# Last Fourier stage in column tiles, spectral products taken from PSUM, one-bank tiles and merged score units, in a kernel that mixes segmented attention with a Fourier filter

## Chip, cores, metric

One core of a Trainium2 chip. The time is the device time of one execution in microseconds (us), lower is better. Engines: PE is TensorE (matmuls), PEld its weight loads, DVE is VectorE, ACT is ScalarE, POOL is GpSimd, SP issues the DMAs. "Granted clock" is the TensorE clock that the throttle let through, as a share of full speed. The state of a run is fast or slow (over 1.5% above the fastest run of the same kernel).

## The reference, cut to what matters

```python
def reference(A_x, A_wq, A_wk, A_wv, A_wo, A_beta, B_x, B_w_r, B_w_i, gate_w):
    # x: (1, 2048, 640) bf16; 32 heads of 20; 4 segments of 512 tokens
    g = sigmoid((x * gate_w).sum(-1, keepdims=True))
    a = _A_ref(x, ...)   # per segment: causal softmax attention inside the segment, mixed with
                         # phi(q) @ M / (phi(q) @ z), where M, z sum phi(k)^T v and phi(k) of the
                         # segments before; phi(t) = t + 1 if t > 0 else exp(t); then @ wo
    b = _B_ref(x, w_r, w_i)  # irfft2(rfft2(x) * (w_r + i w_i)), cast to bf16
    return g * a + (1 - g) * b
```

Two independent computations share the core. Attention has 4 segments x 8 groups of four heads: scores, `exp`, a causal mask, times v. The Fourier part is a chain of matmul stages (called F1, D, T, the product with W, Tb, Db, Fb in the code). The two meet only in the last line.

## The kernel before

The kernel records all its operations, each with a priority in planned microseconds. A list scheduler then plays an execution with estimated costs and fixes the order of each engine's queue and which PSUM bank each tile takes. So a constant in `texp` or `F_START` is not a delay on the chip: it decides what stands in front of what in each in-order queue. PSUM has two pools: banks 0 to 3 are one score tile ("qk"), banks 4 to 7 are for everything else.

```python
    TSTART, TEND = 14.0, 232.0          # planned times of the first and last score unit
    F_START, F_END = 18.0, 160.0        # planned times of the Fourier part
    def texp(self, s, g, u=0):
        return self.TSTART + ((s * 8 + g) * 3 + u) / 96.0 * (self.TEND - self.TSTART)
# ... one group of four heads: three score units, each through the one four-bank tile
            for u, js in enumerate(((0,), (1, 3), (2,))):     # widths 512, 512, 256 per head
                bank = Bank(4, "qk")
                # ... 4 or 8 qk matmuls (row tiles), then
                self.one("act", lambda e: e.activation(ex..., self.ps(bank, 0, [512, 4], [1, width]), ACT.Exp, scale=SC), ...)
                for j in js:
                    self.one("pool", lambda e: e.affine_select(...), 512, ...)      # causal mask
# ... phi: exp on ACT; min(.,1) and max(.,0) and the add on POOL or DVE, whichever the scheduler finds free
            self.Sc.op({"pool": (fmax,) + ts, "dve": (fmax,) + tsd}, ...)
            self.Sc.op({"pool": (fmin,) + ts, "dve": (fmin,) + tsd}, ...)
            self.Sc.op({"pool": (fadd, ...), "dve": (fadd, ...)}, ...)
# ... Fourier part, group g of 16: T in PSUM -> copy to SBUF (Xt) -> products with W on DVE or POOL
                self.Sc.op(self.copy_alts(Xt.ap(ri * 322, [1, KD]), self.ps(bank, 0, [1, KD]), KD), ..., name="ev_T")
            for r in range(2):
                fn = lambda e: e.tensor_tensor(Pt.ap(r * 644, [322, 2], [1, KD]), Xt.ap(0, [322, 2], [1, KD]),
                                               Wt.ap(r * 322, [0, 2], [1, KD]), ALU.mult)        # 642 wide
                self.Sc.op({"dve": (fn, ...), "pool": (fn, ...)}, ..., name="W_mul")
# ... last stage, token residue n2 of 16: full 128-column matmuls give tokens n2, n2+16, n2+32, ...
                for typ in range(2):
                    return (self.ps(bank, 0, [1, 320]), fc.ap(384 if hf and typ else 256, [1, P]),
                            Gt.ap(typ * 322 + 320 * hf, [1 - 2 * hf, 320]), typ == 0, typ == 1, {})
            self.dma(yd[n2::16], ys, ..., name="st_y")           # y to DRAM, strided by 16 tokens
# ... out tile T_ of 128 consecutive tokens
        self.dma(yl, yd[T_ * 128 : ...], [all 16 yd], ..., name="ld_y")    # y back, in token order
        self.one("pool", lambda e: e.tensor_scalar(yl, yl, (1 - g) column, None, ALU.mult), D, ..., name="y_scale")
        # ... 2 x 5 output-projection matmuls, then on DVE: out = psum * g + yl; store
```

(Argument lists, priorities and dependencies are left out where `...` stands.)

The softmax here doesn't subtract the row's maximum and nothing guards it: scores larger than these inputs give would overflow.

Of the kernel before, what the change touches and what calls it, by code (L numbers as in the profile page):

```python
# [10 lines left out]
ALU = mybir.AluOpType  # L11
# [39 lines left out]
class Sched:  # L51
# [9 lines left out]
    def op(self, alts, r=(), w=(), prio=0.0, nbytes=0, name="", tr=False):  # L61
# [14 lines left out]
        for b in r2:  # L76
            dep(b.w)
        for b in w2:
            bb = b
            if isinstance(b, Bank):  # L80
                o.banks.append(b)
                b.ops.append(o)
                bb = b.buf
            dep(bb.w)
            for q in bb.r:
                dep(q)
# [398 lines left out]
class Kern:  # L485
# [56 lines left out]
    def one(self, eng, fn, n, r, w, prio, per=None, fix=None, name=""):  # L542
        fix0, per0 = {"act": (100, 0.833), "dve": (75, 1.04), "pool": (130, 0.86)}[eng]
        per = per0 if per is None else per
        fix = fix0 if fix is None else fix
        return self.Sc.op({eng: (fn, fix + per * n, 90.0)}, r=r, w=w, prio=prio, name=name)

    def dma(self, dst, src, nbytes, r, w, prio, tr=False, name=""):
        def f(e):
            d_, s_ = dst(), src()  # L550
            if tr:
                return e.dma_start_transpose(d_, s_)
            with self.nc.allow_non_contiguous_dma(reason="small strided loads"):
                return e.dma_start(d_, s_)
        return self.Sc.op({"sp": (f, 450.0, 0.0)}, r=r, w=w, prio=prio, nbytes=nbytes, name=name, tr=tr)


    TSTART = 14.0
    TEND = 232.0
    F_START = 18.0  # L560
    F_END = 160.0

    def texp(self, s, g, u=0):
        return self.TSTART + ((s * 8 + g) * 3 + u) / 96.0 * (self.TEND - self.TSTART)

# [13 lines left out]
    def alloc(self):  # L579
# [6 lines left out]
        self.yd = nc.dram_tensor("y_scr", (S, D), BF)  # L586
# [4 lines left out]
        self.Ac = T("Ac", [P, 5 * 2048])  # L591
# [6 lines left out]
        self.Xt = [T(f"Xt{i}", [P, 2 * 322]) for i in range(2)]  # L598
        self.Pt = [T(f"Pt{i}", [P, 4 * 322]) for i in range(1)]
# [3 lines left out]
        late = [self.Ac.off]  # L603

        def TL(name, shape):
# [3 lines left out]
            assert late[0] <= self.fcat.off  # L609
            return t  # L610
        self.Gt = [TL(f"Gt{i}", [P, 2 * 322]) for i in range(2)]
        self.ys = [TL(f"ys{i}", [P, D]) for i in range(2)]
        self.yl = [TL(f"yl{i}", [P, D]) for i in range(3)]
        self.ot = [TL(f"ot{i}", [P, D]) for i in range(3)]
        self.oT = [TL(f"oT{i}", [P, 5 * P]) for i in range(3)]
# [3 lines left out]
        self.WVP = 642  # L619
        self.wv = T("wv", [P, 5 * self.WVP])  # L620
# [11 lines left out]
        self.ex = [T(f"ex{i}", [P, 4 * 1280]) for i in range(self.NEX)]  # L632
# [14 lines left out]
    def after_Ac(self, key):  # L647

        if key in self.seen:
            return []  # L650
        self.seen.add(key)
        return [self.b("Ac", c, nb) for c in range(5) for nb in range(4)]
# [7 lines left out]
    def record(self):  # L660
# [12 lines left out]
        for T_ in range(16):  # L673
            self.finish_tile(T_)

    def loads(self):
# [14 lines left out]
        for q in range(8):  # L691
# [5 lines left out]
        wload(self.wv, self.wv_d, "wv", 3.0, self.WVP)  # L697
        self.dma(lambda: self.wv.ap(640, [self.WVP, 5], [1, 1]), lambda: dap(self.gw_d, 0, [1, P], [P, 5], [1, 1]),
                 P * 5 * 64, [], [self.b("wvg")], 3.1, name="ld_gw")
# [43 lines left out]
    def project(self, s):  # L743
# [4 lines left out]
        lead = 34.0 if s else 14.0  # L748
        t0 = t_end - lead
        span = lead - 8.0 if s else 2.0  # L750
# [20 lines left out]
        for i in range(4):  # L771
            pv = t0 + span * (0.3 + 0.6 * i / 4)
            if s == 0:
                pv = self.TSTART + 1.0 + 1.5 * i
            self.v_tile(s, i, pv, xT, xb)
        z = self.gz
        self.one("act", lambda e: e.activation(z.ap(16 + 4 * s, [1, 4]), z.ap(4 * s, [1, 4]), ACT.Exp, scale=-1.0), 4,
                 [b("gz", s)], [b("ge", s)], t_end + 20.0)
        self.one("dve", lambda e: e.tensor_scalar(z.ap(4 * s, [1, 4]), z.ap(16 + 4 * s, [1, 4]), 1.0, None, ALU.add), 4,
                 [b("ge", s)], [b("gz", s)], t_end + 20.0)  # L780
        self.one("dve", lambda e: e.reciprocal(z.ap(32 + 4 * s, [1, 4]), z.ap(4 * s, [1, 4])), 4,
                 [b("gz", s)], [b("g", s)], t_end + 20.0)
        self.one("dve", lambda e: e.tensor_scalar(z.ap(48 + 4 * s, [1, 4]), z.ap(32 + 4 * s, [1, 4]), -1.0, 1.0, ALU.mult, ALU.add),
                 4, [b("g", s)], [b("omg", s)], t_end + 20.0)

    def proj_tile(self, s, which, t, prio, xT, xb):
# [18 lines left out]
        if (which == "q" and s >= 1) or (which == "k" and s <= 2):  # L805
# [3 lines left out]
            late = prio + 6.0  # L809
# [5 lines left out]
            else:  # L815
# [7 lines left out]
            ts = (130 + 0.86 * L, 90.0)  # L823
            tsd = (75 + 0.3 * L, 85.0)
            self.Sc.op({"pool": (fmax,) + ts, "dve": (fmax,) + tsd}, r=[qb], w=[db] + alias, prio=late, name="phi_max")
            self.Sc.op({"pool": (fmin,) + ts, "dve": (fmin,) + tsd}, r=[], w=[b("et", pi_)], prio=late, name="phi_min")
            self.Sc.op({"pool": (fadd, 130 + 1.72 * L, 90.0), "dve": (fadd, 75 + 0.54 * L, 85.0)}, r=[b("et", pi_)], w=[db], prio=late,
                       name="phi_add")
# [3 lines left out]
    def v_tile(self, s, i, prio, xT, xb):  # L832
        b = self.b
        va, vb = self.va[s % 2], b("va", s % 2, i)
        for (h0, nh, w) in ((0, 25, 500), (25, 7, 141)):
            self.v_part(s, i, h0, nh, w, prio, xT, xb, va, vb)

    def v_part(self, s, i, h0, nh, w, prio, xT, xb, va, vb):
        b = self.b
        bank = Bank(1, "gen")  # L840
        for c in range(5):
            self.mms([(lambda c=c: (self.ps(bank, 0, [1, w]), xT.ap(c * L + i * P, [1, P]), self.wv.ap(c * self.WVP + h0 * DH, [1, w]),
                                    c == 0, c == 4, {}), w)], [b("wv"), b("wvg"), xb, bank], [], prio, name="vproj")
# [3 lines left out]
        if w > nh * DH:  # L847
            self.one("dve", lambda e: e.tensor_copy(self.gz.ap(4 * s + i, [1, 1]), self.ps(bank, nh * DH, [1, 1])), 1,  # L848
                     [bank], [b("gz", s)], prio, name="ev_gate")

# [14 lines left out]
    def mem_read_tile(self, s, i, q, mine):  # L865
        b = self.b
        Mz, mb = self.Mz[s % 2], b("Mz", s % 2)
        prio = self.texp(s, 0) + 2.0 + 2.0 * i
        bank = Bank(1, "gen")
        items = []  # L870
        for n_, (t, h, nh) in enumerate(mine):
# [12 lines left out]
            dn.ap(16, [1, 16], [0, DH]), ALU.mult), 320, [bank, rb], [b("mem", i, q)] + ([b("xr", k) for k in range(8)] if s == 1 else []),  # L884
            prio, name="mem_mul")

    def attend(self, s):
# [3 lines left out]
        for g in range(8):  # L891
            self.attend_group(s, g)
        if s < 3:
            for i in range(4):
                self.dma(lambda i=i: dap(self.od.ap(), (s * L + i * P) * D, [D, P], [1, D]), lambda i=i: on.ap(i * D, [1, D]),
                         P * D * 2, [b("on", s % 2, g) for g in range(8)], [b("od", 4 * s + i)], self.texp(s + 1, 0) + 3.0, name="st_o")

    def attend_group(self, s, g):
        b = self.b
        va = self.va[s % 2]  # L900
        on = self.on[s % 2]
        if True:
            G = s * 8 + g
            ex = self.ex[G % self.NEX]
            exb = lambda j, G=G: b("ex", G % self.NEX, j)
            pidx = (2 * s + g // 4) % self.NPAD
            qp, kp = self.qp[pidx], self.kp[pidx]
            gl = g % 4
            rb = [b("qp", pidx, j) for j in range(4)] + [b("kp", pidx, j) for j in range(4)]
            for u, js in enumerate(((0,), (1, 3), (2,))):  # L910
                prio = self.texp(s, g, u)
                bank = Bank(4, "qk")
                items = []
                width = 0
                for j in js:
                    n = L - P * j
                    for hh in range(4):
                        def th(hh=hh, j=j, n=n, o=width, bank=bank):
                            return (self.ps(bank, hh * 512 + o, [1, n]), kp.ap(gl * L + P * j, [1, P], p0=32 * hh, np_=DH),
                                    qp.ap(gl * L + P * j, [1, n], p0=32 * hh, np_=DH), True, True, {"tile_position": (32 * hh, 0)})  # L920
                        items.append((th, n / 4.0))
                    width += n
                o = self.mms(items, rb + [bank], [], prio - 3.0, name="qk")
                fn, occ, lat = o.alts["pe"]
                o.alts["pe"] = (fn, sum(max(c * PECOL, 13.0) for _, c in items) + 150.0, lat)
                base = JOFF[js[0]]
                self.one("act", lambda e, bank=bank, width=width, base=base, ex=ex: e.activation(  # L927
                    ex.ap(base, [1280, 4], [1, width]), self.ps(bank, 0, [512, 4], [1, width]), ACT.Exp, scale=SC),
                    4 * width, [bank], [exb(j) for j in js], prio - 3.0, name="exp")
                for j in js:  # L930
                    self.one("pool", lambda e, j=j, ex=ex: e.affine_select(  # L931
                        ex.ap(JOFF[j], [1280, 4], [1, P]), ex.ap(JOFF[j], [1280, 4], [1, P]), [[0, 4], [1, P]], ALU.is_ge, 0.0,
                        base=0, channel_multiplier=-1), 512, [], [exb(j)], prio, name="mask")
            prio = self.texp(s, g, 2) + 1.5
# [262 lines left out]
```

## Time and profile before

| | before |
|---|---|
| time, median of 4 runs | 342.0 us (340.3 to 342.38) |
| profiled run | 341.18 us, span 339.5 us, mean clock 0.878 |
| first exp starts, last exp starts | 30.3 us, 318.57 us |
| after the start of the last exp | 20.9 us of the span |
| DMA traffic | 45.42 MB |

The page's first part gives each engine's busy time, its share of the span and its instructions.

```profile
span 339.5 us, 7771 instructions
PE 271.2 (80%) x3052; PEld 153.3 (45%) x3052; DVE 200.0 (59%) x484; ACT 210.7 (62%) x221; POOL 214.7 (63%) x259
```

No engine is full on average, so the average says little. The table by windows (same kernel; columns: window, its length, busy us and instructions of PE, PEld, DVE, ACT and POOL, granted clock, DMA share, GB/s) shows two regimes.

```profile
55.00:100.00 45.00, 40.01 (x442) 21.56 (x442) 36.70 (x87) 31.54 (x37) 29.34 (x37) 0.92 0.63 147
100.00:150.00 50.00, 41.95 (x510) 25.31 (x511) 41.91 (x103) 36.08 (x42) 39.03 (x47) 0.93 0.55 140
150.00:200.00 50.00, 42.00 (x427) 22.42 (x423) 37.05 (x92) 31.90 (x39) 43.23 (x48) 0.92 0.44 109
200.00:250.00 50.00, 49.17 (x577) 28.44 (x576) 33.88 (x89) 39.01 (x45) 21.75 (x34) 0.98 0.30 96
250.00:270.00 20.00, 14.61 (x203) 8.21 (x201) 8.49 (x30) 14.07 (x10) 14.35 (x17) 0.67 0.54 142
270.00:300.00 30.00, 24.09 (x299) 13.45 (x301) 10.58 (x23) 17.26 (x12) 24.11 (x25) 0.82 0.54 134
300.00:320.00 20.00, 11.75 (x159) 6.16 (x158) 5.02 (x11) 12.46 (x8) 18.54 (x21) 0.61 0.22 64
```

Up to 250 us PE does most of the work: 85.5% busy over 55 to 200 us (123.97 of 145), then 49.17 of 50. From 250 us on PE has gaps and a low clock, although the last exp does not start for another 69 us: it is no longer PE that holds the score chain up. The timeline of ACT shows that chain (same kernel; start, duration, what; in brackets the idle time before it and what ended it).

```profile
258.83 1.88 ACT L927 ACTIVATE ex_114<-psum 128x2048 bf16<-128x2048 f32 x1 [0.59 <-PE psum L529]
261.42 1.88 ACT L927 ACTIVATE ex_114<-psum 128x2048 bf16<-128x2048 f32 x1 [0.72 <-PE psum L529]
263.81 1.02 ACT L927 ACTIVATE ex_114<-psum 128x1024 bf16<-128x1024 f32 x1 [0.51 <-PE psum L529]
```

Each exp ends, the next qk matmuls may write the only score tile, and 0.5 to 0.7 us later the next exp starts: 2.59 us from one start to the next. With three exps per group, this chain alone sets the least time that the last quarter can take. Late in the chain POOL is in it too. The chain that ended last (same kernel; start, us, engine, what):

```profile
290.49 4.27 DMA yl_84<-y_scr
294.85 1.88 POOL yl_84 L1148
296.74 1.77 POOL ex_115 L931 x3
298.51 1.87 POOL yl_85 L1148
```

POOL scales a tile of y by (1 - g) in 1.87 us between the masks, after it came back from DRAM. Two more readings of this kernel are used later. First the view by tile of the W products (minimum, median and maximum in ns):

```profile
L1083 DVE TENSOR_TENSOR Pt_67<-Xt_66,Wt_62 x8: 486/600/1644, 83.0 to 180.0; 128x642 bf16<-128x642 bf16 x8
L1083 POOL TENSOR_TENSOR Pt_67<-Xt_66,Wt_62 x8: 1327/1576/1646, 83.1 to 180.9; 128x642 bf16<-128x642 bf16 x8
```

The same DVE product takes 0.49 us or up to 1.64 us. Second, what PE waited for from 55 to 200 us (in total us, times, the longest):

```profile
PE psum L529 <- DVE mem L882: 4.1, 3, 1.9
PE psum L529 <- DVE Bt_63 L539: 3.3, 2, 2.0
PE psum L529 <- DVE on_118 L950: 3.0, 2, 2.5
```

With the shorter lines, waits for DVE are 18 us of these 145.

### The profile page before, as it was taken

Reading aid. Unit: us, or ns where it says so; the run is one execution under the profiler, and the core shown is the slowest. Engines: PE = TensorE matmul, PEld = TensorE weight load, DVE = VectorE, ACT = ScalarE, POOL = GpSimd, SP = SyncE. Lnnn points to the kernel's source line nnn. Section 1 sums busy time; section 2 is a strip of 40 time slices with the busy share of each in tenths; the row PEclk is TensorE's granted clock in tenths of the full one; section 3 lists DMA queues with packets and bytes.
Section 4 is the critical chain, followed back from the end, with each engine's and each line's share of the span. In section 5 each row is a group of like instructions: output and inputs, shape, how many; then the busy total and the mean of one; then the engine's idle time right before and its main releaser. Section 6 shows DMA issues by size and latency. Waiting matters only on the chain.

```text
span 339.5 us, 7771 instructions
## 1 busy us (share of the span) xinstructions
PE 271.2 (80%) x3052; PEld 153.3 (45%) x3052; DVE 200.0 (59%) x484; ACT 210.7 (62%) x221; POOL 214.7 (63%) x259
## 2 busy tenths in 40 slices
PE   0985898988869869896997879999987858867464
PEld 0343645444436436453544435655544434433232
DVE  0153358769997896886768668666573324342113
ACT  1167864776858777763776577788677565574500
POOL 5060336697646867989899753445365859899602
PEclk9999597899997998997999879999997587795559
DMA  7579983497447584352331842241435662660133
GB/s 195 179 241 266 265 209 89 119 239 130 139 127 144 161 200 136 88 159 68 94 99 48 141 143 78 81 135 57 125 95 143 157 156 77 163 168 21 41 69 106
DMA packets 66469, 45.42 MB, mean 134 GB/s; under 512 B 34264, under 2 KB 64248, under 8 KB 66424
## 3 DMA queue, kind: packets, MB, share of 16 engines
q1 hardware_dynamic: 66432, 44.92, 50.3%
q8 instruction: 24, 0.39, 0.5%
q14 instruction: 13, 0.11, 0.2%
HBM read 25.24 MB, written 12.58 MB: 111 GB/s over the span
## 4 chain that ended last, share of the span: by engine, by line
PE 44%; POOL 17%; DVE 16%; ACT 11%; issue 4%; DMA 4%; SPq 1%; DVEq 0%; POOLq 0%
PE psum L529 44%; ACT ex_114 L927 5%; ACT ex_115 L927 3%; DVE Pt_67 L1083 2%; POOL et_103 L820 2%; POOL Pt_67 L1083 2%; POOL ex_115 L931 2%; ACT ex_116 L927 2%; POOL yl_84 L1148 2%; DMA wq<-in_A_wq_dram 2%; POOL et_102 L820 1%; DMA yl_84<-y_scr 1%; POOL ex_116 L931 1%; POOL yl_86 L1148 1%; DVE Cp L539 1%
## 5 line engine op out<-in xcount | busy, mean ns | idle before, releaser
L927 ACT ACTIVATE ex_114<-psum 128x2048 bf16<-128x2048 f32 (+1 forms) x33 | 52.5, 1590 | 17.9 <-PE psum L529 17.9
L927 ACT ACTIVATE ex_115<-psum 128x2048 bf16<-128x2048 f32 (+1 forms) x33 | 52.4, 1589 | 13.7 <-PE psum L529 13.5
L927 ACT ACTIVATE ex_116<-psum 128x2048 bf16<-128x2048 f32 (+1 forms) x30 | 47.8, 1592 | 15.7 <-PE psum L529 15.5
L931 POOL TENSOR_SCALAR_AFFINE_SELECT ex_114<-ex_114 128x512 bf16<-128x512 bf16 x44 | 28.1, 653 | 22.4 <-ACT ex_114 L927 22.4
L931 POOL TENSOR_SCALAR_AFFINE_SELECT ex_115<-ex_115 128x512 bf16<-128x512 bf16 x44 | 28.0, 650 | 19.7 <-ACT ex_115 L927 19.7
L931 POOL TENSOR_SCALAR_AFFINE_SELECT ex_116<-ex_116 128x512 bf16<-128x512 bf16 x40 | 25.9, 660 | 15.9 <-ACT ex_116 L927 15.8
L529 PE MATMUL psum<-qp_108,kp_110 20*128 20x512 bf16 (+3 forms) x256 | 19.7, 343 | 12.5 <-ACT ex_114 L927 7.0
L529 PE MATMUL psum<-big,Ac 128*128 128x321 bf16 x96 | 22.5, 304 | 4.2 <-DVE va_113 L844 2.1
L529 PE MATMUL psum<-xT_97,wq 128*128 128x512 bf16 x50 | 18.4, 444 | 8.9 <-DMA wq<-in_A_wq_dram 8.9
L529 PE MATMUL psum<-qp_109,kp_111 20*128 20x512 bf16 (+3 forms) x256 | 18.8, 329 | 5.3 <-ACT ex_115 L927 2.5
L529 PE MATMUL psum<-wv,xT_98 128*128 128x500 bf16 (+1 forms) x80 | 22.7, 300 | 0.0
L529 PE MATMUL psum<-big,Cp 128*128 128x321 bf16 (+1 forms) x96 | 21.6, 310 | 0.2
L529 PE MATMUL psum<-xT_98,wq 128*128 128x512 bf16 x50 | 19.4, 444 | 0.5 <-DVE on_118 L950 0.5
L529 PE MATMUL psum<-wo,oT_90 128*128 128x320 bf16 x60 | 15.4, 374 | 4.9 <-DMA oT_90<-on_118 4.3
L529 PE MATMUL psum<-wv,xT_97 128*128 128x500 bf16 (+1 forms) x80 | 18.9, 311 | 0.5 <-DVE gz L848 0.5
L820 POOL TENSOR_SCALAR et_102<-et_102 128x512 bf16<-128x512 bf16 x6 | 8.9, 1487 | 15.3 <-ACT et_102 L810 15.3
L529 PE MATMUL psum<-xT_98,wk 128*128 128x512 bf16 x50 | 18.0, 379 | 0.0
L1148 POOL TENSOR_SCALAR yl_84<-yl_84,gz 128x640 bf16<-128x640 bf16 x6 | 11.3, 1885 | 10.2 <-DMA yl_84<-y_scr 10.2
L529 PE MATMUL psum<-xT_97,wk 128*128 128x512 bf16 x50 | 16.8, 379 | 0.0
L954 POOL TENSOR_TENSOR on_118<-on_118,mem 128x320 bf16<-128x320 bf16 x16 | 12.7, 792 | 5.4 <-DVE on_118 L950 5.4
L529 PEld LDWEIGHTS psum<-qp_108,kp_110 20*128 20x128 bf16 x256 | 5.3, 94 | 23.5 <-ACT ex_114 L927 9.1
L1083 POOL TENSOR_TENSOR Pt_67<-Xt_66,Wt_62 128x642 bf16<-128x642 bf16 x8 | 12.4, 1545 | 4.9 <-ACT Xt_66 L537 3.7
(209 smaller groups left out, 711.6 us busy)
## 6 DMA issues: line engine op xcount, KB each, us to landing
xsb<-in_A_x_dram SPq DMA_DIRECT2D x8, 320.0 KB, 4.0
qp_108<-q_scr SPq DMA_DIRECT2D x16, 128.0 KB, 2.6
kp_110<-k_scr SPq DMA_DIRECT2D x16, 128.0 KB, 3.2
qp_109<-q_scr SPq DMA_DIRECT2D x16, 128.0 KB, 3.0
kp_111<-k_scr SPq DMA_DIRECT2D x16, 128.0 KB, 3.9
tt_58<-tab_tt SPq DMA_DIRECT2D x6, 256.0 KB, 3.1
tt_59<-tab_tt SPq DMA_DIRECT2D x5, 256.0 KB, 3.1
tt_60<-tab_tt SPq DMA_DIRECT2D x5, 256.0 KB, 3.1
```

The source lines that it names most:

```text
L529: h = e.matmul(o_, l_, r_, start=st, stop=sp_, **kw)
L539: alts["dve"] = (lambda e: e.tensor_copy(dst(), src()), 75 + 1.04 * n, 85.0)
L820: fmin = lambda e: e.tensor_scalar(et.ap(0, [1, L]), et.ap(0, [1, L]), 1.0, None, ALU.min)
L927: self.one("act", lambda e, bank=bank, width=width, base=base, ex=ex: e.activation(ex.ap(base, [1280, 4], [1, width]), self.ps(bank, 0, [5 ...
L931: self.one("pool", lambda e, j=j, ex=ex: e.affine_select(ex.ap(JOFF[j], [1280, 4], [1, P]), ex.ap(JOFF[j], [1280, 4], [1, P]), [[0, 4], [1 ...
L954: self.one("pool", lambda e, g=g: e.tensor_tensor(on.ap(80 * g, [D, 4], [1, 80]), on.ap(80 * g, [D, 4], [1, 80]), self.mem.ap(80 * g, [D, ...
L1083: fn = lambda e, r=r, Pt=Pt, Xt=Xt, Wt=Wt: e.tensor_tensor(Pt.ap(r * 644, [322, 2], [1, KD]), Xt.ap(0, [322, 2], [1, KD]), Wt.ap(r * 322, ...
L1148: self.one("pool", lambda e: e.tensor_scalar(yl.ap(0, [1, D]), yl.ap(0, [1, D]), self.gz.ap(48 + T_, [1, 1]), None, ALU.mult), D, [b("omg" ...
```

## The change

Intent: take y out of DRAM, relieve POOL, and spread the Fourier work so that TensorE has something to do beside the score chain until the end. Five parts:

1. **Last stage in column tiles.** The last Fourier matmul gets 32 columns for each of four column tiles instead of 128. One out tile then holds 32 tokens of each of four residues, in the permuted order in which y arises. Attention tiles are put in the same order (o is stored or sliced with a stride), so y goes from PSUM with its scaling by (1 - g) on ACT or DVE straight to the final sum. No y store, no y load, no POOL scaling. The gate is computed by one-column matmuls in the same token order.
2. **W products from PSUM.** DVE multiplies T by W directly out of PSUM, four 321-wide products per group; the sums go to POOL alone.
3. **phi**: max and min on DVE alone, the add on POOL alone.
4. **Merged score units**: five 2048-wide exps for two groups instead of four 2048-wide and two 1024-wide.
5. **Order**: the Fourier part is planned over 24.9 to 227.6 instead of 18 to 160, with new constants for leads and lags. The diff also changes what the scheduler is told that some operations cost (adds on POOL from 130 + 1.72 to 100 + 1.95 ns per element, phi's steps on DVE) and some buffer rules.

"One-bank tiles" are the last-stage and projection tiles that each take one PSUM bank. The diff's core (cut at `...`):

```diff
-    TSTART = 14.0
-    TEND = 232.0
-    F_START = 18.0
-    F_END = 160.0
+    TSTART, TEND, F_START, F_END = 18.5, 227.8, 24.9, 227.6
+    LEAD, LEAD_END, QK_LEAD, PV_LAG = 25.2, 2.6, 24.8, -3.5
+    PH, MEM0, MEMU, O_BASE = 4.0, 10.8, 1.0, 5.0
+    O_STEP, FIN = 5.6, (3.0, 1.0)
+    UNITS = (((0, (0,)),), ((0, (1, 3)),), ((1, (0,)),), ((0, (2,)), (1, (2,))), ((1, (1, 3)),))
...
-        self.Pt = [T(f"Pt{i}", [P, 4 * 322]) for i in range(1)]
+        self.Pt = [T(f"Pt{i}", [P, 4 * 322]) for i in range(2)]
...
+    def gate(self, s, t_end, xT, xb):
+        for a in range(4):
+            for c in range(5):
+                for q in range(4):
+                        return (self.ps(bank, a, [1, 1], p0=32 * q, np_=32), xT.ap(c * L + 4 * a + q, [16, 32]), self.gw.ap(c, [1, 1]),
+                                c == 0, c == 4, {"tile_position": (0, 32 * q)})
...
-            self.Sc.op({"pool": (fmax,) + ts, "dve": (fmax,) + tsd}, ...)
-            self.Sc.op({"pool": (fmin,) + ts, "dve": (fmin,) + tsd}, ...)
-            self.Sc.op({"pool": (fadd, ...), "dve": (fadd, ...)}, ...)
+            self.Sc.op({"dve": (fmax,) + tsd}, ...)
+            self.Sc.op({"dve": (fmin,) + tsd}, ...)
+            self.Sc.op({"pool": (fadd, 100 + 1.95 * L, 90.0)}, ...)
...
-                self.Sc.op(self.copy_alts(... Xt.ap(ri * 322, [1, KD]) ...), name="ev_T")
-            for r in range(2):
-                fn = lambda e: e.tensor_tensor(Pt.ap(r * 644, ...), Xt.ap(0, ...), Wt.ap(r * 322, ...), ALU.mult)
-                self.Sc.op({"dve": (fn, ...), "pool": (fn, ...)}, ..., name="W_mul")
+                for r in range(2):
+                    self.one("dve", lambda e: e.tensor_tensor(
+                        Pt.ap((2 * r + ri) * 322, [1, KD]), self.ps(bank, 0, [1, KD]), Wt.ap(r * 322, [1, KD]), ALU.mult), KD, ..., name="W_mul")
...
-            self.dma(... self.yd ..., name="st_y")
-        self.dma(... yl ..., name="ld_y")
-        self.one("pool", lambda e: e.tensor_scalar(yl, yl, ..., None, ALU.mult), D, ..., name="y_scale")
+            for typ in range(2):
+                for q in range(4):
+                        return (self.ps(bank, 0, [1, 320], p0=32 * q, np_=32), self.fcat.ap((384 if hf and typ else 256) + 32 * s, [1, 32]),
+                                self.G.ap((4 * a + q) * 644 + typ * 322 + 320 * hf, [1 - 2 * hf, 320]), typ == 0, typ == 1,
+                                {"tile_position": (0, 32 * q)})
+            self.Sc.op({"act": (... ACT.Copy, scale=gcol(48) ...), "dve": (... tensor_scalar ... gcol(48) ...)}, ..., name="ev_Fb")
...
-        self.dma(lambda: dap(self.out, T_ * P * D, [D, P], [1, D]), ...)
+        self.dma(lambda: dap(self.out, (s * L + 4 * a) * D, [D, 4], [16 * D, 32], [1, D]), ...)
```

## The prediction

> **What bounds the kernel now.** No single engine (page, part 1: PE 271.2 of 339.5 us busy, POOL 214.7, ACT 210.7, DVE 200.0), but two regimes, seen in the table by windows and the start times of the exps:
>
> - 30 to 250 us: TensorE, busy 84 to 98% from 55 us on, granted clock 0.86 to 0.98. Two groups of four heads take 15 to 26 us.
> - 250 to 319 us: the serial score chain. One four-bank tile passes between qk matmuls and exp: start to start 2.6 us for a 2048-wide exp (1.88 us itself), 1.4 to 2.4 us for a 1024-wide one. Two groups take 14.4 to 15.5 us though PE has spare time (39 of 50 us busy, clock 0.76, then 0.60). POOL is loaded too: 19.1 of the 22 us from 300 on, with y scalings of 1.885 us between the masks.
>
> Then 21 us after the last exp; 9 us of loads stand before the first matmul.
>
> **What changes: instruction counts of both programs times durations of the trace.**
>
> - POOL: loses 16 y scalings (30 us), 15 wide W products (22.5) and 16 phi min/max (24); gains 18 phi adds at 1.15 us and 19 W adds at 0.78. Net -41: near 174 us.
> - ACT: 80 exps of 1.88 us instead of 64 and 32 halves (151 against 153 us: nothing by itself), but 80 handoffs of about 0.65 us instead of 96. It loses 11 T evictions and others: near 198 us.
> - DVE: loses 21 T evictions, 17 products, 19 W adds, 18 phi adds; gains 64 PSUM products (estimate 0.48 us, as other 321-wide PSUM reads). Near 193 us.
> - PE: 64 last-stage matmuls become 256 of 32 columns. The Trainium skill, "TensorEngine Tiling (Array Packing)", Key Properties, says different tiles run in parallel; this trace agrees for two 64-column tiles (F1 pairs start every 55 ns, as one full matmul does). So 35 ns each, 9 us in all: no gain, no loss. 320 one-column gate matmuls are new: 6 to 10 us.
> - DMA: 32 transfers of y (5.2 MB) vanish, with the 4.3 us wait for y that the chain shows.
>
> **On the critical path.** Mainly order. Before, the Fourier work is crowded into groups 1 to 22 and the last ten groups run on the score chain. After, it is spread to group 28, and output tiles run beside the last exps. From unit costs at full clock (0.22 us per 512-column matmul, 0.033 per pv matmul and so on) PE has, per two groups, 4 to 17 us before and 8 to 16 after, plus 2.2 for qk. Divided by the 0.82 efficiency of the first regime, with a floor of 13.3 us, the 16 pairs sum to about 255 us. With 29 us before the first exp and 22 after the last: **306 us**, range 291 to 322. Chances: faster by over 2% 0.94, within 2% 0.05, slower 0.01.
>
> **What would show each step.** 80 exps, 2.6 us apart where unhindered; POOL near 174 us; no y traffic; the 256 matmuls near 9 to 12 us together; PE share 85 to 90%, clock above 0.7 in the last quarter; last exp near 283 us instead of 319; tail unchanged.
>
> **What would make it wrong.** Column tiles not running four at once (256 x 138 ns would cost 26 us more, and 16 in the last output projection); slow strided weight loads in gate and last projection; banks held longer by products behind a busy DVE; W adds waiting behind masks on POOL; an efficiency below 0.82, then 320 or more.

## The result, and the profile after

| | before | after |
|---|---|---|
| time, median of 4 runs | 342.0 us (340.3 to 342.38) | 297.73 us (294.61 to 298.14) |
| profiled run: time, span, clock | 341.18, 339.5, 0.878 | 294.61, 292.9, 0.968 |
| first exp starts | 30.3 us | 31.45 us |
| last exp starts | 318.57 us | 263.69 us |
| from there to the end of the span | 20.9 us | 29.2 us |
| DMA traffic | 45.42 MB | 40.24 MB |

The two starts of the last exp, first of the kernel before, then of the kernel after:

```profile
318.57 1.02 ACT L927 ACTIVATE ex_115<-psum 128x1024 bf16<-128x1024 f32 x1 [0.51 <-PE psum L529]
```

```profile
263.69 1.88 ACT L963 ACTIVATE ex<-psum 128x2048 bf16<-128x2048 f32 x1 [0.73 <-PE psum L534]
```

The ratio of fast runs is 0.8694, with a 95% interval of 0.8628 to 0.876. Ratios here are the mean time of one kernel's fast runs over that of the other's of the same rounds, so not quite the ratio of the medians quoted. One caution for all that follows: the profiled run of the kernel after is the fastest of its four (clock 0.968; the other three had 0.934 to 0.941 and 297.4 to 298.1 us). Its trace flatters the typical run by about 3 us.

The page's first part, and below it the table by windows, of the kernel after:

```profile
span 292.9 us, 8858 instructions
PE 255.4 (87%) x3684; PEld 149.9 (51%) x3684; DVE 193.9 (66%) x485; ACT 198.9 (68%) x182; POOL 170.3 (58%) x249
```

```profile
55.00:100.00 45.00, 40.35 (x567) 22.26 (x564) 32.54 (x76) 34.82 (x32) 33.76 (x48) 0.96 0.67 168
100.00:150.00 50.00, 47.34 (x640) 27.79 (x638) 44.89 (x117) 40.30 (x35) 43.92 (x62) 1.00 0.52 141
150.00:200.00 50.00, 43.90 (x650) 25.75 (x646) 40.85 (x111) 37.40 (x31) 39.38 (x58) 1.00 0.43 122
200.00:250.00 50.00, 49.42 (x718) 28.06 (x721) 35.20 (x92) 38.12 (x30) 24.93 (x37) 0.97 0.32 76
250.00:270.00 20.00, 20.00 (x348) 11.45 (x344) 12.43 (x28) 12.96 (x12) 9.06 (x14) 1.00 0.75 111
270.00:300.00 30.00, 14.16 (x278) 9.66 (x272) 8.15 (x16) 5.45 (x11) 0.24 (x1) 0.93 0.28 72
```

The gap in the last quarter is gone: PE is busy for all of 250 to 270 us, at full clock. The middle is better as well: 131.58 of 145 us busy over 55 to 200 us (90.7%, before 85.5%), at a mean clock of 0.99 instead of 0.92. Part of this belongs to the fast profiled run: in n1 and e6 below, which do the same work (profiled at 299.4 and 299.7 us), the same stretch shows 128.76 and 127.35 us (88 to 89%) at 0.94 and 0.96. The start times of the exps say where the time went: the first half of the exps took 160.2 us before and 121.2 after, the second half 128.1 and 111.0. So 39 of the 56 us by which the score chain got shorter lie in its first half, not in the last quarter. The chain that ended last has turned into one long run of matmuls (kernel after):

```profile
234.51 41.84 PE psum L534 x659
276.73 4.04 DMA out_dram<-ot_83
281.90 4.01 DMA out_dram<-ot_83
```

Two stores of output tiles are its last long pieces. The waits of PE from 55 to 200 us (kernel after) have shrunk, those for DVE to 7.5 us in all (5.1 in n1, 7.5 in e6):

```profile
PE psum L534 <- DVE Bt_64 L544: 2.1, 2, 1.7
PE psum L534 <- DVE on_114 L993: 1.9, 2, 1.5
```

And the view by tile of the W products (kernel after) shows one duration instead of a spread:

```profile
L1123 DVE TENSOR_TENSOR Pt_67<-psum,Wt_63 x32: 446/481/496, 89.1 to 192.2; 128x321 bf16<-128x321 f32 x32
```

Why the spread before? The Trainium skill, "SBUF — State Buffer", section "Who interferes with whom", says that DVE and POOL share a port pair as an exclusive lock, and that a DVE operation with two SBUF inputs contends with a POOL operation that reads SBUF, while one with at most one SBUF input, outside the two-port modes, does not. This trace agrees where both engines run products: a DVE product with both inputs in SBUF took 0.50 us where it began first (106.75 us, POOL's own at 106.80), and 1.64 us where POOL had begun its own just before (timeline of the kernel before):

```profile
97.83 1.43 POOL L1083 TENSOR_TENSOR Pt_67<-Xt_66,Wt_62 128x642 bf16<-128x642 bf16 x1 [3.72 <-ACT Xt_66 L537]
97.97 1.64 DVE L1083 TENSOR_TENSOR Pt_67<-Xt_66,Wt_62 128x642 bf16<-128x642 bf16 x1
```

It does not agree for every POOL operation that reads SBUF: in three cases POOL's one-input TENSOR_SCALAR was under way (as from 179.45 to 180.93 us), and the DVE product (at 179.99 us) still took 0.49 to 0.50 us. With one input in PSUM the longest of 32 is 0.496 us. The skill's "VectorE: DVE Perf Modes" (section "The perf-mode tier table") gives a two-input operation on bf16 twice the plain rate with both inputs in SBUF, and the plain rate with one in PSUM; the trace agrees, with 642 elements in 0.49 us there and 321 in 0.48 us here. The change pays twice the element time on DVE and gets a duration that POOL does not disturb.

### The profile page after: what moved, and what is told of

It is laid out like the page before. It is cut to its first block, busy times and chain, and to the rows that moved or that the text cites. A ratio compares the mean times of both kernels' runs of the same rounds, so it can differ in the third digit from the quotient of the medians.

```text
span 292.9 us, 8858 instructions
## 1 busy us (share of the span) xinstructions
PE 255.4 (87%) x3684; PEld 149.9 (51%) x3684; DVE 193.9 (66%) x485; ACT 198.9 (68%) x182; POOL 170.3 (58%) x249
## 2 busy tenths in 40 slices
DMA packets 61576, 40.24 MB, mean 137 GB/s; under 512 B 33464, under 2 KB 59352, under 8 KB 61528
## 4 chain that ended last, share of the span: by engine, by line
PE 54%; DVE 16%; DMA 9%; ACT 9%; POOL 6%; issue 3%; SPq 1%; DVEq 0%; POOLq 0%
PE psum L534 54%; ACT ex L963 7%; DMA out_dram<-ot_83 3%; DMA q_scr<-qu_99 2%; DVE Pt_67 L1123 2%; DMA wq<-in_A_wq_dram 2%; POOL ex L966 2%; DMA pkn<-phk_105 1%; DVE Cp L544 1%; POOL Yt_69 L1128 1%; POOL phq L853 1%; DVE phq L852 1%; DVE et_101 L851 1%; DVE et_102 L851 1%; DMA kp_109<-k_scr 1%
## 5 line engine op out<-in xcount | busy, mean ns | idle before, releaser
L963 ACT ACTIVATE ex<-psum 128x2048 bf16<-128x2048 f32 x80 | 150.1, 1876 | 34.9 <-PE psum L534 34.5
L966 POOL TENSOR_SCALAR_AFFINE_SELECT ex<-ex 128x512 bf16<-128x512 bf16 x128 | 80.3, 644 | 57.9 <-ACT ex L963 56.3
L534 PE MATMUL psum<-va_111,ex 128*128 128x21 bf16 x640 | 25.6, 173 | 3.7 <-DVE on_114 L993 1.5
L534 PEld LDWEIGHTS psum<-va_111,ex 128*128 128x128 bf16 x640 | 22.8, 97 | 11.4 <-DVE on_114 L993 2.5
L534 PEld LDWEIGHTS psum<-va_112,ex 128*128 128x128 bf16 x640 | 23.0, 96 | 6.8 <-issue 2.4
L534 PE MATMUL psum<-va_112,ex 128*128 128x21 bf16 x640 | 25.6, 173 | 0.0
L534 PE MATMUL psum<-qp_107,kp_109 20*128 20x128 bf16 (+3 forms) x256 | 16.9, 319 | 7.2 <-ACT ex L963 5.7
L544 DVE CAST Cp<-psum 65x256 bf16<-65x256 f32 (+1 forms) x29 | 15.0, 543 | 5.0 <-PE psum L534 4.9
L544 DVE CAST G<-psum 128x321 bf16<-128x321 f32 x28 | 13.3, 491 | 5.3 <-PE psum L534 5.0
L534 PE MATMUL psum<-qp_108,kp_110 20*128 20x128 bf16 (+3 forms) x256 | 15.8, 301 | 0.1
L853 POOL TENSOR_TENSOR phk_104<-phk_104,et_101 128x512 bf16<-128x512 bf16 x6 | 6.9, 1153 | 14.9 <-DVE et_101 L851 14.9
L1128 POOL TENSOR_TENSOR Yt_68<-Pt_66 128x321 bf16<-128x321 bf16 x16 | 11.5, 731 | 5.9 <-DVE Pt_66 L1123 4.8
L1123 DVE TENSOR_TENSOR Pt_66<-psum,Wt_62 128x321 bf16<-128x321 f32 x32 | 14.4, 481 | 0.7 <-PE psum L534 0.6
```

The costliest lines, as they stand in the source:

```text
L534: h = e.matmul(o_, l_, r_, start=st, stop=sp_, **kw)
L544: alts["dve"] = (lambda e: e.tensor_copy(dst(), src()), 75 + 1.04 * n, 85.0)
L853: fadd = lambda e: e.tensor_tensor(dst(), dst(), et.ap(0, [1, L]), ALU.add)
L963: self.one("act", lambda e: e.activation(dst(), src(), ACT.Exp, scale=SC), 4 * width, [bank], [self.exb(s, g, j) for g, j in outs], prio - ...
L966: self.one("pool", lambda e, g=g, j=j: e.affine_select(self.ex.ap(self.exo(s, g) + JOFF[j], [1280, 4], [1, P]), self.ex.ap(self.exo(s, g) ...
L1123: self.one("dve", lambda e, r=r, ri=ri, Pt=Pt, Wt=Wt, bank=bank: e.tensor_tensor(Pt.ap((2 * r + ri) * 322, [1, KD]), self.ps(bank, 0, [1, ...
```

## The experiments

That the kernel is faster needed no defence, but "mainly order", which the prediction claimed, did. Three theories:

- **A, order**: before, the Fourier work is used up too early; feeding it evenly beside the score chain is most of the gain.
- **B, side work**: the gain comes from what no longer has to be done or waited for: y through DRAM and POOL, wide W products, phi on POOL, a sixth of the exps.
- **C, clock**: the low granted clock of 250 to 320 us itself makes the score chain slow; the gain there comes from the higher clock, and any busy PE would get it.

Each kernel gave a correct result. "After" and "before" say which kernel the edit starts from. All ratios are to the kernel before of the same rounds; before had medians of 342.4 to 342.9 us on these chips.

### e1: after, with the Fourier work crowded early again

```diff
-    TSTART, TEND, F_START, F_END = 18.5, 227.8, 24.9, 227.6
+    TSTART, TEND, F_START, F_END = 18.5, 227.8, 18.0, 160.0
-    PH, MEM0, MEMU, O_BASE = 4.0, 10.8, 1.0, 5.0
+    PH, MEM0, MEMU, O_BASE = 4.0, 10.8, 1.0, 72.6
```

(The second line keeps the output tiles at their planned times.)

> The kernel after, with the Fourier work due as early as before (start 18, end 160 on the priority scale instead of 24.9 and 227.6; output tiles keep their own due times). Theory A, the spread order is the main gain: gives back at least 20 of the 44 us, 318 us or more. Rival B, the gain is the new way of y (no trip through DRAM, no scaling on POOL) and the order hardly matters: 302 us or less. My guess between them is 306, since output tiles can now fill the late stretch in place of Fourier work.

Measured: median 312.87 us (308.11 to 314.8). Two of the four runs counted as slow; the two fast ones are 308.11 and 311.48. The last exp starts at 281.9 us instead of 263.7. The table by windows of this kernel:

```profile
250.00:270.00 20.00, 19.98 (x325) 10.78 (x325) 13.61 (x28) 15.97 (x12) 8.36 (x13) 1.00 0.68 100
270.00:282.00 12.00, 10.66 (x185) 5.83 (x185) 8.01 (x17) 8.31 (x6) 5.79 (x9) 0.99 0.19 59
282.00:300.00 18.00, 8.27 (x179) 6.56 (x180) 2.97 (x7) 2.54 (x3) 3.47 (x6) 0.53 0.21 46
```

PE is busy nearly until the last exp here (before: until 250 us) and goes hungry only behind it, at a clock of 0.53. So the old symptom, a score chain without side work, does not come back. What early order costs lies in the crowded half: the first 40 exps take 143.7 us instead of 121.2, the last 40 108.2 instead of 111.0. By its fast runs (mean 309.8 us, before 341.6 in these rounds: 0.907) order is worth about 13 of the 44.7 us that 0.8694 means at 342 us; with the slow runs counted in, about 15. The time lies between what the two theories expected: A holds, for under a third of the gain.

### b3: before, with the Fourier work spread, and nothing else

```diff
-    F_START = 18.0
-    F_END = 160.0
+    F_START = 24.9
+    F_END = 227.6
```

> The kernel before with the late Fourier order alone (24.9 to 227.6). Theory A says that order matters by itself: faster than before by 10 us or more, 332 or less, although all but 18 of the 160 output projection matmuls then come after the last score matmuls (22 us at full clock, with y scalings of 1.9 us each beside them). If the order pays only with the column tiles: 340 us or more. Guess 330, from the last exp near 280 us plus a tail of 48.

Measured: median 339.41 us, ratio 0.9901 (0.9837 to 0.9965). A clear miss, and the most useful run. The last exp starts at 283.0 us, 35.6 us earlier than before: the score chain is sped up as A said. But 55.0 us of the span follow it, instead of 20.9. What was waited for from 283 us on (engine, line, what; total us, times, longest):

```profile
DVE ot L1165 <- POOL yl L1148: 20.0, 5, 6.7
POOL yl L1148 <- DMA yl<-y_scr: 19.4, 8, 4.1
```

With the old path every out tile needs all 16 residues of y, because the last transposition through DRAM mixes them. If the Fourier part ends late, all sixteen out tiles come after it, each with a load and 1.88 us of POOL. So 34 of the 35.6 us are handed back in the tail. In this kernel order pays only with a path for y that can end late.

### e7 and e8: after, with the old path of y; late and early order

The new kernel, but full-width last-stage matmuls, y to DRAM and back, POOL scaling, out tiles of consecutive tokens. e7 keeps the new order; e8 is e7 with the Fourier part planned over 18 to 160.

```diff
+                for typ in range(2):
+                    return (self.ps(bank, 0, [1, 320]), fc.ap(384 if hf and typ else 256, [1, P]),
+                            self.G.ap(n2 * 644 + typ * 322 + 320 * hf, [1 - 2 * hf, 320]), typ == 0, typ == 1, {})
+            self.dma(yd[n2::16], ys, ..., name="st_y")
+        self.dma(yl, yd[T_ * 128 : ...], ..., name="ld_y")
+        self.one("pool", lambda e: e.tensor_scalar(yl, yl, gz column, None, ALU.mult), D, ..., name="y_scale")
-        ... column-tile matmuls and scaled evictions in finish_tile, permuted o, strided out store
e8:
-    TSTART, TEND, F_START, F_END = 18.5, 227.8, 24.9, 227.6
+    TSTART, TEND, F_START, F_END = 18.5, 227.8, 18.0, 160.0
```

> The kernel after, but y goes the old way: last Fourier stage on full tiles per n2, through DRAM, scaled on POOL, output tiles of natural tokens; Fourier order late as in the kernel after. All 160 output projection matmuls then stand after the last scores (by the program's order), 22 us at 0.138 us each, plus the landing of y and 16 scalings of 1.9 us on POOL: 320 to 332 us whichever theory holds, with the last exp near 265 us as now. If the way of y is unimportant: under 305.

Measured: median 309.53 us, ratio 0.9041 (0.8964 to 0.9118). The expectation of 320 or more missed: the last exp starts at 264.66, as in the kernel after, and the tail is 43.5 us instead of 29.2. The tail is long in the way of b3, but the waits in it are smaller; from 264 us on:

```profile
DVE ot L1202 <- POOL yl L1185: 16.8, 12, 1.6
...
POOL yl L1185 <- DMA yl<-y_scr: 5.9, 11, 0.8
```

The loads of y now run mostly ahead; what the sums wait for is POOL's scaling. What else of the change shortens the tail from b3's 55.0 to 43.5 us was not taken apart. One difference is what the scheduler is told: in e7 a scaling costs 100 + 2.8 x 640 = 1892 ns, in b3 and before 130 + 0.86 x 640 = 680 ns.

> As the last, but with the early Fourier order (18 to 160), which lets y be ready for the late stretch: the best setting for the old way. Against e1_crowded (same order, new way of y) it costs: theory B 15 us or more; theory A under 6 us. Guess 312 us.

Measured: median 320.4 us, ratio 0.9369 (0.9303 to 0.9435); last exp at 297.4 us. My estimate was 8 us too low. Beside e1 it costs about 10 us (0.030 of 342), between the 6 of theory A and the 15 of theory B. Beside e7, early order costs 11 us (0.0328 of 342), near the 13 of e1; beside the kernel after, both undone cost 0.0675 of 342, 23 us. So order and the path of y are worth about 12 us each and add up here within the scatter, with the rest of the change in place.

### e3: after, with the scaling of y on POOL

```diff
-            self.Sc.op({"act": (... ACT.Copy, scale=gcol(48) ...), "dve": (... tensor_scalar, gcol(48) ...)}, ..., name="ev_Fb")
+            self.Sc.op(self.copy_alts(ys..., psum..., 320), ..., name="ev_Fb")
+        self.one("pool", lambda e: e.tensor_scalar(ys.ap(0, [1, D]), ys.ap(0, [1, D]), gcol(48), None, ALU.mult), D, ..., name="y_scale")
```

> The kernel after with the scaling of y put back on POOL (16 operations of about 1.9 us between the last stage and the sum; the eviction is a plain copy), the rest of the new way kept. Theory B (relief of POOL): 308 us or more, masks waiting behind scalings in the last quarter as before. Otherwise POOL goes from 170 to 200 us and nothing else moves: under 302 us. Guess 301.

Measured: median 302.48 us, ratio 0.8851 (0.8785 to 0.8918), about 5 us slower than the kernel after, at the upper end of what I expected. POOL is back at 199.8 us. So of the 12 us for y's path, about 5 are POOL's scaling, and the rest is what else e7 puts back, the trip through DRAM and the full tiles.

### e5: after, with phi on POOL or DVE again

```diff
-            self.Sc.op({"dve": (fmax,) + tsd}, ...)
-            self.Sc.op({"dve": (fmin,) + tsd}, ...)
-            self.Sc.op({"pool": (fadd, 100 + 1.95 * L, 90.0)}, ...)
+            self.Sc.op({"pool": (fmax,) + ts, "dve": (fmax,) + tsd}, ...)     # ts = 130 + 0.86 L, as before
+            self.Sc.op({"pool": (fmin,) + ts, "dve": (fmin,) + tsd}, ...)
+            self.Sc.op({"pool": (fadd, 130 + 1.72 * L, 90.0), "dve": (fadd, 75 + 0.54 * L, 85.0)}, ...)
```

> The kernel after with phi free to take DVE or POOL as before (19 min/max on POOL at 1.5 us instead of DVE at 0.5, 22 adds on DVE instead of POOL): POOL about +28-26, DVE about +3. Slow POOL minima sit on the path to mem reads and memory updates and delay masks: guess 301 us; within 2 us of 298 would mean that the assignment of phi is worth nothing.

Measured: median 305.61 us, ratio 0.8946 (0.8877 to 0.9016), 8 to 9 us slower, over twice what I expected. POOL's total hardly rose (173.3 against 170.3 us). So it is not POOL's total load. The groups of POOL (this kernel; busy us, mean ns, idle before it):

```profile
L851 POOL TENSOR_SCALAR et<-et 128x512 bf16<-128x512 bf16 x11 | 16.5, 1502 | 17.6 <-ACT et L841 17.4
L852 POOL TENSOR_SCALAR phq<-qu 128x512 bf16<-128x512 bf16 x6 | 9.0, 1504 | 1.1 <-DVE qu L544 1.1
```

The scheduler was told that such a step takes 130 + 0.86 x 512 = 570 ns on POOL; it takes 1500. So it placed 19 of them there as if they were cheap, and its plan was off behind each. PE's waits from 55 to 200 us now include 4.0 us for the transposed phi(k) and 2.8 us for masks on POOL (0.8 and 0.3 in the kernel after). These waits fit the reading that slow steps in the wrong place are the cause, but they do not show it: a kernel with POOL allowed and its cost corrected was not run, and e5 also tells another cost for phi on DVE (229 ns, 358 in the kernel after) and moves 22 adds to DVE.

### e4: after, with the old W step

```diff
-                for r in range(2):
-                    self.one("dve", ... tensor_tensor(Pt..., psum 321, Wt...), ..., name="W_mul")
+                self.Sc.op(self.copy_alts(Xt..., psum..., KD), ..., name="ev_T")
+            for r in range(2):
+                self.Sc.op({"dve": (fn 642 wide, ...), "pool": (fn, ...)}, ..., name="W_mul")
-                self.Sc.op({"pool": (W_add, ...)}, ...)
+                self.Sc.op({"dve": (W_add, ...), "pool": (W_add, ...)}, ...)
```

(One Pt tile instead of two, as before.)

> The kernel after with the W step of before: T evicted to SBUF, wide products on DVE or POOL, one product buffer, adds on DVE or POOL. Adds 32 evictions (14 us of ACT and DVE), takes 64 PSUM products (31 us of DVE) away, adds about 25 us of DVE and 20 of POOL back; the bank of T is released after one 0.45 us read instead of two. If that step is worth something here: 303 to 310 us, by a longer chain per Fourier group; if the spread order hides it: within 3 us of 298. Guess 303.

Measured: median 301.82 us, ratio 0.8816 (0.8739 to 0.8893), about 4 us slower than the kernel after. The interval overlaps a little with that of the kernel after (0.8628 to 0.876), and only three runs are fast, so the size is uncertain. Its profiled run was slow (305.5 us), so its trace is used for no difference here.

### e2: after, with 96 score units instead of 80

```diff
-    UNITS = (((0, (0,)),), ((0, (1, 3)),), ((1, (0,)),), ((0, (2,)), (1, (2,))), ((1, (1, 3)),))
+    UNITS = (((0, (0,)),), ((0, (1, 3)),), ((0, (2,)),), ((1, (0,)),), ((1, (1, 3)),), ((1, (2,)),))
```

> The kernel after with the score units of before: 96 (64 of 2048 and 32 of 1024 columns) instead of 80. If the score chain still bounds it: 16 more handoffs of 0.5 to 0.65 us, 306 us or more. If TensorE bounds it (busy 97 to 100% from 200 us on): the chain has slack, under 301 us. Guess 302.

Measured: median 298.62 us, ratio 0.8733 (0.8666 to 0.88): merging is worth about 1 us, within the scatter. The expectation's second case (under 301 us) holds: the score chain has slack in the kernel after. That PE is the bound there is read from the tables (49.42 of 50 and 20.00 of 20 us busy from 200 to 270 us).

### n1: after, with a scheduler constant nudged

```diff
-    HOP = 70.0
+    HOP = 75.0
```

The constant is an assumed delay between engines; about half of the queue positions change, and no work does.

> A control: the kernel after with one constant of its scheduler's model moved (hop between engines 75 instead of 70 ns). No operation changes, only the static order of about half the rows. It measures how much of the single-part differences (0.9, 4.1, 4.8, 7.9 us so far) may be luck of the order: within 2 us of 298 they stand; 3 us or more off and those under that size can't be told from luck.

Measured: median 296.97 us, ratio 0.8692 (0.8633 to 0.875). Another order of the same work moves the time by under 1 us, so the differences of 4 us and more above are hardly luck of the order; but this is one nudge, not a spread of many.

### b2: before, with 120 useless matmuls in the last ten groups

```diff
+            if s * 8 + g >= 22:
+                # behind each score unit: two tiles of two 512-wide matmuls, whose result nobody reads
+                self.mms(fit, [exb(js[0]), b("fcat"), fbank], [], self.texp(s, g, u) + 300.0, name="fill")
```

> The kernel before plus 120 useless matmuls of 512 columns (26 us of TensorE at full clock) of lowest priority from group 22 on, in the stretch where TensorE had spare time and a granted clock of 0.76 to 0.6. Theory C, the low clock itself costs several us there: granted clock over 0.9 in 250 to 320 us, exp start to start 2.4 instead of 2.6 us, and the kernel 4 to 10 us faster than before (332 to 338). Rival: the clock only follows idleness and costs nothing; the fillers get in the way, 342 to 352 us.

Measured: median 346.89 us, ratio 1.0149 (1.0095 to 1.0203). The table by windows of this kernel, to be set beside the same three lines of before:

```profile
250.00:270.00 20.00, 17.69 (x217) 9.42 (x219) 9.95 (x36) 13.11 (x12) 13.81 (x17) 1.00 0.55 130
270.00:300.00 30.00, 26.95 (x315) 15.12 (x315) 11.34 (x24) 17.14 (x11) 25.63 (x26) 1.00 0.58 150
300.00:320.00 20.00, 19.24 (x235) 10.17 (x238) 5.37 (x12) 13.79 (x9) 16.31 (x20) 1.00 0.23 66
```

The clock rose from 0.67, 0.82 and 0.61 to 1.00, and the score chain did not get faster: the last exp starts at 320.9 us (before 318.6), and 2048-wide exps follow each other after 2.65 us (2.59). The 4 to 10 us that theory C expected did not appear, so keeping PE busy is not by itself a gain here, and the low clock goes with the gaps of PE. A small cost of the clock is not excluded: from 255 to 318 us the 512-wide qk matmuls took 0.38 us instead of 0.47, and the fillers, which stand in the same queue, may have eaten that. The Trainium skill, "TensorE: Matmul & The Clock Gate", section "What's actually happening", says that the clock follows how busy PE has been recently; these two tables agree.

### e6: after, with the queue order of the column tiles turned

```diff
-            for typ in range(2):
-                for q in range(4):
+            for q in range(4):
+                for typ in range(2):
```

Now the two matmuls of one column tile stand one behind the other in the queue instead of four apart. If tiles overlapped only when neighbours in the queue differ, this would cost.

> The kernel after with the last Fourier stage's loop turned: the two matmuls of one column tile one after the other, then the next tile, instead of the four tiles in turn. If tiles run in parallel only when neighbours in the queue are different tiles, eight matmuls take about 5 x 138 ns = 0.69 us instead of 0.28: 0.41 us more in 32 places, 13 us of TensorE, and since TensorE is full from 200 us on, the kernel is 8 to 13 us slower (306 to 311). If a queue of four covers any order: no change.

Measured: median 297.71 us, ratio 0.8679 (0.8616 to 0.8743): nothing changed, the expectation missed. Groups by form, first of the kernel after, then of e6:

```profile
L534 PE MATMUL psum<-G,fcat 128*32 128x320 bf16 x256 | 13.6, 303 | 0.3 <-DVE ot_83 L1219 0.3
```

```profile
L534 PE MATMUL psum<-G,fcat 128*32 128x320 bf16 x256 | 13.8, 304 | 0.3 <-DVE ot L1219 0.3
```

In the timeline a group of 8 takes 0.46 us in the kernel after (0.47 in e6) and 24 in a row take 1.00 (1.01): 16 more in 0.54 us, 34 ns each. One such matmul alone spans 0.30 us, so they overlap in either order.

### e9: after, with more tiles for the end and the last segment's projections last

The trace of the kernel after shows DVE waiting 3.02 us at 280.87 us for an earlier store to free its tile, so I gave y and the sums six tiles each and moved the last segment's projections behind all other last-stage work.

```diff
-        self.ys = [TL(f"ys{i}", [P, D]) for i in range(3)]
-        self.ot = [TL(f"ot{i}", [P, D]) for i in range(3)]
+        self.ys = [3 tiles as before] + [3 more in the space of Cp]
+        self.ot = [3 tiles as before] + [3 more in the space of Cp]
+        if s == 3:
+            prio += 30.0
```

> Aims at the tail of the kernel after (PE waits 1.3 us for the transposes of the last segment, and a sum waits 3.0 us for its output tile to be stored): six y and six output tiles instead of three, and the last segment's projections placed behind all others. Tail from the last exp's start to the end 30.0 us now; expect 27 to 28.5, the kernel 1.5 to 3 us faster, 295 to 296.5.

Measured in five rounds: median 299.52 us, ratio 0.8737 (0.8688 to 0.8787), not faster; the expectation missed. Its profiled run was slow (302.13 us), so only its kind of wait is read here, the end of its chain:

```profile
276.71 1.21 SPq L557
...
281.00 4.19 DMA oTl<-on
285.43 5.82 PE psum L534 x153
```

The wait for the tile is gone and another stands in its place. The last segment's attention output must be transposed by four DMAs, issued one after another, before 160 projection matmuls; nothing else is left to hide that. No experiment beat the kernel after by more than the scatter.

## Why the prediction was right or wrong

Direction, size and range were right: 297.73 us lies in 291 to 322, 8 us under the 306 predicted. Point by point:

| predicted | measured |
|---|---|
| POOL near 174, ACT near 198, DVE near 193 us | 170.3, 198.9, 193.9 |
| PE share 85 to 90%, clock of the last quarter above 0.7 | 87%; 0.93 or more in every window |
| 80 exps of 1.88 us | 80 of 1.876 us mean |
| 256 last-stage matmuls, 35 ns each, "9 to 12 us together" | 34 ns each, but 13.6 us busy |
| 320 gate matmuls, 6 to 10 us | 5.6 us |
| first exp after 29 us | 31.45 us |
| the 16 pairs sum to 255 us | 232.2 us (first to last exp) |
| last exp near 283 us | 263.7 us |
| tail 22 us, "unchanged" | 29.2 us, and 1.7 from span to device time |
| "mainly order" | 11 to 13 of 44.7 us |

The profiled run's sum is 31.45 + 232.24 + 29.21 + 1.7 = 294.6 us. Against 29 + 255 + 22 the errors are +2.5, -22.8 and +8.9. They cancel in part: that the total is better than its terms is luck.

**The mis-sized term is the 255 us for the pairs**, at "the 0.82 efficiency of the first regime". That efficiency was read from the kernel before and held constant. It is no constant of the kernel. Busy share of PE times clock is 0.871 x 0.93 = 0.81 before (30 to 250 us) and 0.917 x 0.96 = 0.88 after (first to last exp). In n1 and e6 it is 0.90 x 0.94 = 0.85, and their score chains took 236.9 and 238.0 us. With 0.88 for 0.82 the 255 would have been 238 where 232.2 was measured; with 0.85 it would have been 246 where 237 to 238 was measured (estimates, as if every pair were bound by PE). So the efficiency explains about 17 of the 22.8 us in the profiled run, but only about half of the miss in the two others; the rest, in the work counted or in the floor, stays open.

I had counted the removed DVE and POOL time well, and then let none of it reach the critical path, which was to be "mainly order". Part of it was there as waits: PE's waits for DVE fell from 18 to 7.5 us from 55 to 200 us. What raised the clock in that stretch is not shown. Undone one at a time, phi costs 8 to 9 us (e5), the W step 4 (e4), POOL's scaling 5 (e3), and merging about 1 (e2).

**The tail was mis-sized too.** I took it as unchanged, but spreading work to the end moves work behind the last exp. When the last qk matmuls were done, PE's queue still held 112 last-stage and 210 projection matmuls and 80 of the attention; PE is busy with them to 285.8 us. Two lines of the timeline of the kernel after show what the end waits for:

```profile
278.31 0.64 PE L534 MATMUL psum<-wo,oTl 128*32 128x320 bf16 x12 [1.31 <-DMA oTl<-on_115]
280.87 1.01 DVE L1219 SCALAR_TENSOR_TENSOR ot_83<-psum,gz,ys_80 128x320 bf16<-128x320 f32 x2 [3.02 <-DMA out_dram<-ot_83]
```

e9 tried to shorten it and only exchanged the wait.

**"Mainly order" was the wrong account of the gain.** By e1, and by e8 against e7, order is worth 11 to 13 us with the rest in place, the path of y about 12 (e7), phi 8 to 9, W 4, merging 1: some 38 of 44.7 us, if these add, as only order and y were shown to do. Order alone, in the kernel before, is worth 1% (b3): it moved the last exp forward by 35.6 us, and the old path of y took 34 back. The picture of the last quarter was right, but most of the shortening lies before it (39 of 56 us in the first half of the exps). What failed for order alone is the step from "the last exp comes earlier" to "the kernel ends earlier".

**The risk named first, column tiles that do not overlap, did not occur.** The Trainium skill, "TensorEngine Tiling (Array Packing)", Key Properties, says that tiles run in parallel, and both queue orders did (e6). The figure of 9 to 12 us for the 256 matmuls mixed a pace with a busy time: each group of 8 ends with a pipeline's tail in which the profile still counts PE as busy (0.46 us, of which 8 x 34 ns is 0.27). The 64 full matmuls before took 13.5 us by the same measure, so "no gain, no loss" holds. The strided weight loads did come slower (158 ns in the gate and 141 in the last projection, 95 for the other 32-column loads), with no cost seen: the 320 gate matmuls kept under the 6 to 10 us foreseen.

Open: how much of the gain in the middle is the higher clock of 55 to 200 us itself (b2 tested the late stretch only), the exact size of e1, whose runs scatter by 6.7 us, and the remaining 7 us or so, which may lie in the other planning constants and told costs or in parts that do not add.

## What to carry to other kernels

Removing a late bottleneck by reordering helps only if what comes behind it can also end late: before spreading work, ask which step needs all of it, as the trip of y through DRAM did. Don't carry an engine's efficiency from the old trace into the new one when the change takes away the waits that made it: read which waits go, and raise it by them. Where a scheduler decides, check the costs it is told: a step told as 570 ns that takes 1500 went with 8 to 9 us in e5, though no run shows that the wrong cost alone did it.

## What the Trainium skill lacked or had wrong

- "GPSIMD Engine Reference", section "4.1 Engine selection", calls one-input elementwise work on GPSIMD "roughly line-rate". Here a one-input TENSOR_SCALAR on POOL took 1.50 us for 512 bf16 elements per partition and 1.885 us for 640, about 2.9 ns an element, while a two-input TENSOR_TENSOR of 512 took 1.15 us (2.3 ns an element). The one-input operation was the slower one. It is not so of every one-input operation: the mask (TENSOR_SCALAR_AFFINE_SELECT) took 0.64 us for 512.
- "TensorEngine Tiling (Array Packing)", section "Instruction Overhead", says that a matmul with one free column has the latency of one with 60. Latency is not pace: in the kernel after, 80 one-column matmuls spread over four column tiles ran in 1.41 us, under 18 ns each, which is also under the 25 ns from start to start that "TensorE: Matmul & The Clock Gate", section "Wait — 56ns, not 53.3ns?", gives as the least. On the full array the floor does show: in the attention 16 matmuls of 21 columns took 0.55 us where 12 took 0.45, 25 ns each. Whether it holds within one column tile, no run here shows.
- "SBUF — State Buffer", section "Who interferes with whom", says of any POOL operation that reads SBUF that a DVE operation with two SBUF inputs contends with it. In the kernel before that holds for products on POOL (1.64 us for 0.50), but not for the one-input TENSOR_SCALAR of phi: three DVE products that began while one was under way took 0.49, 0.50 and 0.49 us.
- "TensorEngine Tiling (Array Packing)" does not say whether neighbours in the queue must be on different tiles to overlap. With four tiles they need not: 8 matmuls took 0.46 us with tiles alternating and 0.47 us with two in a row on each tile.
